# Weight bits put together in a PSUM bank, head pairs 5 to 7 on one bank by groups, and small VectorE work of pairs 4 to 7 on ScalarE

## The chip, the cores and the metric

One NeuronCore of a Trainium2 chip runs the whole kernel. Its engines work side by side, each through its own queue in order: TensorE (PE in the profile; PEld is its weight loads), VectorE (DVE), ScalarE (ACT), GpSimd (POOL) and the load queue of SyncE (SP). The metric is the device time of one execution in microseconds; the median of the runs counts.

## The reference

Three stages follow each other. Causal attention in a window comes first (4 batches, 8 heads, 576 positions, 64 values a head; heads 0 to 3 see 32 positions, heads 4 to 7 every fourth of 128). Its output, 2304 tokens of 512 values, goes through a first layer whose weights are float64, and then through a layer of 8 experts of which each token uses two.

```python
scores = scale * np.matmul(q, k.transpose(0, 1, 3, 2))
scores = np.where(masks[None, :, :, :], scores, -1000000000.0)
...
attn = attn / (np.sum(attn, axis=-1, keepdims=True) + 1e-09)
x = np.matmul(attn, v)        # then as 2304 tokens of 512
...
h = x @ w_in                  # w_in, w_out are float64
g = h * np.cos(h)
x = g @ w_out
...
noisy_logits = logits + noise_scale * noise
top2 = np.argpartition(-noisy_logits, 2, axis=1)[:, :2]
...
        h = np.maximum(x[mask] @ w1[e], 0.0)
        out[mask] += top2_w[mask, k, None] * (h @ w2[e])
```

## The kernel before

**Attention** works on 16 head pairs (`u`), 4 for each batch. A pair's queries lie block-diagonal, so one product serves both heads. `a_scores` writes a pair's masked scores as two groups of 5 and 4 blocks of 96 columns, each in one PSUM bank (`sc`), and takes the row maxima (L442), scaled by -0.125 (L444). `a_exp` makes the nine exponentials on ScalarE (L459) and their sums, `a_norm` divides (L470, L471, GpSimd L473). `a_part` has three parts: two transpose groups of three blocks (`mt`, copied out to `at` by L487), then the first half of the output (`mo`) and the third transpose group, then the second output half. The output halves are copied into `xraw` by L512 (plain pairs) or L521 (dilated pairs, which reorder the columns). Pairs 0 to 3 and the scores of pair 4 are done in an opening stretch; pairs 4 to 7 lie beside the first layer's steps 0 to 15.

**The first layer** takes blocks of 256 tokens and eighths `p` of the hidden width; a step is one such pair. Steps 0 to 15 serve blocks 0 and 1 in turn, so that a new weight tile is needed every second step; from step 16 on the weights stay. A step is 24 products `ph` (`g1`, L561), then `post` on the other engines (ScalarE L569, VectorE L570, ScalarE Sin L572 and Square L573, VectorE L574, ScalarE L577, GpSimd L578), and 12 products `acc` (`g2`, L588) in two halves that use the result of two steps earlier.

**The weights.** The chip has no float64, so the two 32-bit words of each weight are loaded and cut to float32. A weight tile has four quarters of 128x512. For each, `w_bits` makes three VectorE passes over integers: L289 takes exponent and upper bits out of the high word, L290 puts the sign in, L291 puts in the top of the low word. Their result is the SBUF tile `cut`. Then `w_parts` makes the two parts that TensorE multiplies: a rounded copy on ScalarE (L297) and the remainder on GpSimd (L298).

**PSUM** has eight banks: four for `acc`, two for `ph`, and two (`mid`) that the scores of pairs 5 and on, the transposes and the outputs of pairs 4 and on take in turn.

**The order** is written out by hand. `OPENING` lists the opening stretch. `BESIDE` lists for each step what is issued at its positions: -1 behind `g1`, 0 and 1 behind the first half of `g2` with a stage of `post` after each, 2 behind the second half. Every engine's queue follows this order.

## Time and profile before

| | us |
|---|---|
| median of 3 runs | 1040.83 (1040.08 to 1043.03) |
| span of the profiled execution, first to last instruction | 1039.2 |
| TensorE busy in it | 991.0 |
| VectorE busy | 551.7 |
| ScalarE busy | 461.8 |
| GpSimd busy | 369.4 |

The profiled execution's own time is known as its span; the runs of the table were timed apart from it, and their median lies 1.6 us above. Busy time of an engine can overlap that of the others, so the rows don't add up to the span. PE's busy share is an average over the opening stretch, the first layer (to about 550 us) and the experts, which have different limits.

### The profile page before, as it was taken

The page shows a single profiled execution, that of the slowest core. Times are in us where ns is not written, and L with a number is a line of the kernel's source. Part 1 is how long each engine was busy: PE and PEld are TensorE (multiplying, and loading weights), DVE is VectorE, ACT ScalarE, POOL GpSimd, SP SyncE. Part 2 cuts the span into 40 slices and gives each one's busy share as a digit, 9 for nine tenths or more (in the row PEclk, how much of TensorE's full clock was granted, in tenths as well). Part 3 has the DMA queues.
Part 4 walks back from the last instruction along what each step waited for, and adds up shares of the span by engine and source line. Part 5 has one row for each costly group of instructions (what it writes and reads, how often), then busy time and mean ns, then how long its engine had stood idle before and what let it go on. Part 6 is the DMA issues. An engine that isn't in the chain of part 4 may idle for free.

```text
span 1039.2 us, 16801 instructions
## 1 busy us (share of the span) xinstructions
PE 991.0 (95%) x6560; PEld 879.4 (85%) x6560; DVE 551.7 (53%) x1134; ACT 461.8 (44%) x908; POOL 369.4 (36%) x477
## 2 busy tenths in 40 slices
PE   8787889999999899999999899999999999999995
PEld 6676778988889789888887799898998989898984
DVE  7799885367745645354474656353443435353221
ACT  6646665555646655455564334232332314142110
POOL 5555553243353342423425332322313142323211
PEclk9898999999999999999999899999999999999998
DMA  9962212223312120000145154443533342441201
GB/s 208 334 210 86 80 55 43 85 71 113 95 52 57 46 48 1 21 19 4 35 179 179 26 176 136 159 149 135 166 110 138 123 152 79 163 142 59 64 28 41
DMA packets 70842, 105.71 MB, mean 102 GB/s; under 512 B 31364, under 2 KB 44932, under 8 KB 70753
## 3 DMA queue, kind: packets, MB, share of 16 engines
q1 hardware_dynamic: 60400, 76.33, 24.1%
q0 software_dynamic: 10352, 28.20, 8.7%
q8 instruction: 54, 0.88, 0.4%
q14 instruction: 36, 0.29, 0.1%
HBM read 86.40 MB, written 20.11 MB: 102 GB/s over the span
## 4 chain that ended last, share of the span: by engine, by line
PE 75%; DVE 10%; DMA 5%; ACT 5%; issue 2%; SPq 2%; POOL 1%; POOLq 0%; ACTq 0%; DVEq 0%
PE ye L932 21%; PE pe L899 20%; PE ph L561 14%; PE acc L588 13%; DMA raw<-in_wm 3%; DVE cut L290 2%; PE mgx L882 2%; PE sc L429 1%; PE mo L504 1%; DVE r L570 1%; DVE po L653 1%; PE mt L484 1%; DMA ahead<-in_v 1%; ACT s L459 1%; ACT r L573 1%
## 5 line engine op out<-in xcount | busy, mean ns | idle before, releaser
L561 PE MATMUL ph<-xhl,wm 128*128 128x256 f32 x1728 | 229.5, 289 | 11.4 <-ACT wm L297 4.1
L561 PEld LDWEIGHTS ph<-xhl,wm 128*128 128x128 f32 x1728 | 219.0, 195 | 19.8 <-ACT wm L297 4.5
L932 PE MATMUL ye<-we,h 128*128 128x512 f32 x960 | 232.5, 399 | 0.0
L588 PE MATMUL acc<-wm,g 128*128 128x512 f32 x864 | 219.9, 398 | 2.7 <-POOL wm L298 0.9
L932 PEld LDWEIGHTS ye<-we,h 128*128 128x128 f32 x960 | 179.8, 190 | 39.1
L588 PEld LDWEIGHTS acc<-wm,g 128*128 128x128 f32 x864 | 156.5, 190 | 33.4 <-POOL g L578 1.2
L578 POOL TENSOR_TENSOR g<-r,g 128x512 fp32r<-128x512 f32 x72 | 95.8, 1330 | 209.0 <-ACT g L577 208.9
L899 PE MATMUL pe<-xga,we 128*128 128x384 f32 x768 | 135.9, 335 | 0.0
L899 PEld LDWEIGHTS pe<-xga,we 128*128 128x128 f32 x768 | 132.9, 188 | 0.5 <-issue 0.4
L944 POOL DMA_INDIRECT out<-old,tir x35 | 35.9, 1025 | 232.3 <-DVE old L942 227.8
L902 DVE SCALAR_TENSOR_TENSOR h<-pe,h 128x256 fp32r<-128x256 f32 (+1 forms) x128 | 62.8, 491 | 104.3 <-ACT h L901 103.4
L901 ACT ACTIVATE h<-pe 128x256 fp32r<-128x256 f32 (+1 forms) x128 | 56.1, 438 | 128.7 <-PE pe L899 128.7
L942 DVE SCALAR_TENSOR_TENSOR old<-ye,wts,old 128x512 f32<-128x512 f32 x35 | 26.3, 751 | 134.4 <-PE ye L932 134.4
L899 PE MATMUL pe<-xgb,we 128*128 128x256 f32 x768 | 94.3, 283 | 0.1
L899 PEld LDWEIGHTS pe<-xgb,we 128*128 128x128 f32 x768 | 93.3, 191 | 0.4 <-DVE xgb L885 0.4
L574 DVE SCALAR_TENSOR_TENSOR r<-r,ph 128x512 f32<-128x512 f32 x72 | 49.4, 687 | 82.2 <-ACT r L573 82.1
L570 DVE SCALAR_TENSOR_TENSOR r<-r,ph 128x512 f32<-128x512 int32 x72 | 49.2, 683 | 81.7 <-ACT r L569 81.7
L819 DVE TENSOR_TENSOR we<-wraw,we 128x512 fp32r<-128x512 f32 x121 | 84.3, 705 | 3.6 <-ACT we L818 0.9
L818 ACT ACTIVATE we<-wraw 128x512 fp32r<-128x512 f32 x128 | 78.4, 623 | 2.6 <-issue 2.6
L572 ACT ACTIVATE r<-r 128x512 f32<-128x512 f32 x72 | 45.5, 632 | 65.7 <-DVE r L570 65.6
L569 ACT ACTIVATE r<-ph 128x512 int32<-128x512 f32 x72 | 42.6, 592 | 50.6 <-PE ph L561 50.0
L577 ACT ACTIVATE g<-r 128x512 fp32r<-128x512 f32 x72 | 45.5, 632 | 43.8 <-DVE r L574 29.8
(181 smaller groups left out, 1039.1 us busy)
## 6 DMA issues: line engine op xcount, KB each, us to landing
wraw<-in_we SPq DMA_DIRECT2D x64, 512.0 KB, 5.9
raw<-in_wm SPq DMA_DIRECT2D x28, 512.0 KB, 9.3
vts<-in_v SPq DMA_DIRECT2D x13, 384.0 KB, 3.9
x1d<-x SPq DMA_DIRECT2D x9, 512.0 KB, 3.2
out<-zt SPq DMA_DIRECT2D x18, 256.0 KB, 4.0
kts<-in_kT SPq DMA_DIRECT2D x13, 288.0 KB, 3.4
qts<-in_qT SPq DMA_DIRECT2D x26, 144.0 KB, 3.8
piece<-in_wm SPq DMA_DIRECT2D x4, 512.0 KB, 4.8
```

The costliest lines, as they stand in the source:

```text
L561: nc.tensor.matmul(ph[:, j, :], w[:, a, o:o + P], t[:, x, c, :], start=(c == 0 and n == 0 and (j == 0 or len(cs) == 4)), stop=(c == 3 and ...
L570: nc.vector.scalar_tensor_tensor(r, n, -TWO_PI, ph, op0=ALU.mult, op1=ALU.add)
L572: nc.scalar.activation(r, r, AF.Sin, scale=0.5)
L574: nc.vector.scalar_tensor_tensor(r, r, 0.5, ph, op0=ALU.subtract, op1=ALU.mult)
L578: nc.gpsimd.tensor_tensor(g[:, 1, :], r, g[:, 0, :].bitcast(F32), op=ALU.subtract)
L588: nc.tensor.matmul(ACC[blk][t], g[:, a, j * TB + t * P:j * TB + (t + 1) * P], w[:, x, 1024 + j * DM:1024 + (j + 1) * DM], start=(p == 0 an ...
L818: nc.scalar.activation(t[:, 0, fs], raw, AF.Copy)
L819: eng.tensor_tensor(t[:, 1, fs], raw, t[:, 0, fs].bitcast(F32), op=ALU.subtract)
L899: nc.tensor.matmul(ph[:, :n], w[:, a, o:o + P], x[:, b, c, :], start=(c == 0 and i == 0), stop=(c == 3 and i == 2))
L901: nc.scalar.activation(h[:, 0, f, :], ph[:, :n], AF.Relu)
L902: nc.vector.scalar_tensor_tensor(h[:, 1, f, :], ph[:, :n], 0.0, h[:, 0, f, :].bitcast(F32), op0=ALU.max, op1=ALU.subtract)
L932: nc.tensor.matmul(acc, h[:, a, f, o:o + P], w[:, b, (f % 4) * DM:(f % 4 + 1) * DM], start=(f == 0 and i == 0), stop=(f == 7 and i == 2))
```

## The change

In steps 0 to 15, the stretch marked by the list `alone`, one of the two `mid` banks is given to `w_bits`. Its first two passes then write the bits to this bank (`bits`), and the third reads them there and writes `cut` in SBUF. In the opening and from step 16 on, the two banks go in turn to whoever asks (`mid_tile`), as the two buffers did, and the bits of the four quarters made in the opening stay in SBUF. In steps 0 to 15 everything else that used the two banks has one. The scores and exponentials of pairs 5 to 7 are issued by group (`a_s`, `a_e`), so that the second group's products can stand behind the first group's exponentials. For pairs 4 to 7 the scaling of the maxima and both output copies are issued on ScalarE.

```diff
+    turn = [0]
+    alone = []
+    def mid_tile(name):
+        turn[0] += not alone
+        return psum.tile([P, 512], F32, tag="mid" if alone or turn[0] % 2 else "cut", name=name, bufs=1)
...
-        V.tensor_scalar(t, hw, 3, 0x3FFFFFF8, op0=ALU.logical_shift_left, op1=ALU.bitwise_and)
-        V.scalar_tensor_tensor(t, hw, 0xC0000000, t, op0=ALU.bitwise_and, op1=ALU.bitwise_or)
-        V.scalar_tensor_tensor(t, lw, 29, t, op0=ALU.logical_shift_right, op1=ALU.bitwise_or)
+        b = psum.tile([P, 512], F32, tag="cut", name=f"bits{j}_{k}", bufs=1).bitcast(U32) if alone else t
+        V.tensor_scalar(b, hw, 3, 0x3FFFFFF8, op0=ALU.logical_shift_left, op1=ALU.bitwise_and)
+        V.scalar_tensor_tensor(b, hw, 0xC0000000, b, op0=ALU.bitwise_and, op1=ALU.bitwise_or)
+        V.scalar_tensor_tensor(t, lw, 29, b, op0=ALU.logical_shift_right, op1=ALU.bitwise_or)
...
-    def a_scores(u):
+    def a_scores(u, gs=(0, 1)):
...
-            sc = psum.tile([P, 512], F32, tag=tag, name=f"sc{u}_{g}", bufs=bufs)
+            if u > 4:
+                sc = mid_tile(f"sc{u}_{g}")
+            else:
+                tag, bufs = ("ph", 2) if u == 2 else ("acc", 4)
+                sc = psum.tile([P, 512], F32, tag=tag, name=f"sc{u}_{g}", bufs=bufs)
...
-                nc.vector.tensor_scalar(mx[:, i0:i1], mx[:, i0:i1], -0.125, None, op0=ALU.mult)
+                if u < 4:
+                    nc.vector.tensor_scalar(mx[:, i0:i1], mx[:, i0:i1], -0.125, None, op0=ALU.mult)
+                else:
+                    nc.scalar.activation(mx[:, i0:i1], mx[:, i0:i1], AF.Copy, scale=-0.125)
...
-        mid = psum.tile([P, 512], F32, tag="mid", name=f"mt{u}_{c}", bufs=2)
+        mid = mid_tile(f"mt{u}_{c}")
...
-            a_av(u, 0)
+            a_av(u, 0, u < FUSED)
             a_trans(u, 2)
         else:
-            a_av(u, 1)
+            a_av(u, 1, u < FUSED)
...
+        if i == 0:
+            alone.append(True)
+        if i == 16:
+            alone.clear()
...
-8:0 a_loadv(6) w_parts(4,3) w_bits(5,0) a_scores(6)
-8:1 a_loadqk(7) w_bits(5,1) w_parts(5,0) a_exp(6) a_norm(6) w_parts(5,1) w_piece(7,0) w_bits(5,2)
+8:0 a_loadv(6) w_parts(4,3) w_bits(5,0) a_s(6,0) a_e(6,0)
+8:1 a_s(6,1) a_loadqk(7) w_bits(5,1) w_parts(5,0) a_e(6,1) a_norm(6) w_parts(5,1) w_piece(7,0) w_bits(5,2)
```

What this does to the queues is shown at three places. The number at the end of a name counts buffers and differs between the kernels; `[waits ...]` names the engines whose signal an instruction waits for.

TensorE at the scores of pair 6, step 8 (`sc_0` and `sc_1` are the two groups, `acc_1` the second half of `g2`). Before:

```order
L420 MATMUL sc_0_1233<-mask_113,identb 128x480 [waits PE_49]
L429 MATMUL sc_0_1233<-kts,qts 128x96 [waits DMAHW4_49,DMAHW3_49,DMAHW2_49]
L429 MATMUL sc_0_1233<-kts,qts 128x96 x4
L420 LDWEIGHTS identb
L420 MATMUL sc_1_1242<-mask_113,identb 128x384 [waits DVE_49]
L429 MATMUL sc_1_1242<-kts,qts 128x96 x4
L588 MATMUL acc_1_721<-wm_898,g_3_1083 128x512 x6
```

Now:

```order
L438 MATMUL sc_0_1250<-mask_113,identb 128x480 [waits Activation_49]
L447 MATMUL sc_0_1250<-kts,qts 128x96 [waits DMAHW4_49,DMAHW3_49,DMAHW2_49]
L447 MATMUL sc_0_1250<-kts,qts 128x96 x4
L438 LDWEIGHTS identb [waits DVE_49]
L438 MATMUL sc_1_1268<-mask_113,identb 128x384 [waits Activation_49]
L447 MATMUL sc_1_1268<-kts,qts 128x96 x4
L609 MATMUL acc_1_725<-wm_906,g_3_1096 128x512 x6
```

The order of the products is the same for pairs 6 and 7; the second group waits for VectorE's maximum and for ScalarE's exponentials of the first. For pair 5 alone the six `acc` products moved between the groups.

TensorE at the first transposes of pair 6, behind step 9 (`mt_0` and `mt_1` are the transpose groups, `ph_5` the next step's `g1`). Before:

```order
L484 MATMUL mt_0_1345<-ident,s_1231 96x128 [waits Activation_49,Pool_49]
L484 MATMUL mt_0_1345<-ident,s_1231 96x128 x2
L484 MATMUL mt_1_1351<-ident,s_1231 96x128 [waits DVE_49,Activation_49,Pool_49]
L484 MATMUL mt_1_1351<-ident,s_1231 96x128 x2
L561 MATMUL ph_5_1356<-xhl_448,wm_1226 128x256 [waits DVE_49]
```

Now:

```order
L505 MATMUL mt_0_1365<-ident,s_1248 96x128 [waits Activation_49,Pool_49]
L505 MATMUL mt_0_1365<-ident,s_1248 96x128 x2
L505 MATMUL mt_1_1371<-ident,s_1248 96x128 [waits Activation_49,Pool_49]
L505 MATMUL mt_1_1371<-ident,s_1248 96x128 x2
L582 MATMUL ph_5_1376<-xhl_448,wm_1242 128x256 x8
```

Nothing moved here; the ScalarE signal that `mt_1` waits for was that of the second score group's exponentials, and is now the copy of `mt_0`, the last user of the bank.

ScalarE from the exponentials of pair 6 (`s` from `sc`) on, step 8. Before:

```order
L459 ACT_TABLE_LOAD
L459 ACTIVATE s_1231,sm_1262<-sc_0_1233,mx_1232 128x96 x5
L459 ACTIVATE s_1231,sm_1262<-sc_1_1242,mx_1232 128x96 x4
L297 ACTIVATE wm_1226<-cut_1_1256 128x512
L577 ACTIVATE g_4_1285<-r_4_1213 128x512
L569 ACTIVATE r_4_1319<-ph_4_1294 128x512
L572 ACT_TABLE_LOAD
```

Now:

```order
L465 ACTIVATE mx_1249<-mx_1249 128x5
L481 ACT_TABLE_LOAD
L481 ACTIVATE s_1248,sm_1259<-sc_0_1250,mx_1249 128x96 x5
L593 ACT_TABLE_LOAD
L593 ACTIVATE r_4_1229<-r_4_1229 128x512
L594 ACTIVATE r_4_1229<-r_4_1229 128x512
L465 ACTIVATE mx_1249<-mx_1249 128x4
L307 ACTIVATE wm_1242<-cut_0_1243 128x512
L481 ACT_TABLE_LOAD
L481 ACTIVATE s_1248,sm_1259<-sc_1_1268,mx_1249 128x96 x4
L307 ACTIVATE wm_1242<-cut_1_1279 128x512
L598 ACTIVATE g_4_1304<-r_4_1229 128x512
```

Sin and Square of step 8 (now L593, L594), which stood ahead of all nine exponentials, stand between the two groups; the table load ahead of the next step's Sin follows in both kernels, so pairs 6 and 7 have four loads each in place of two.

## Rows read from the trace of the kernel before

**Rows 1.** The page's first line, and TensorE's part of its first section.

```profile
span 1039.2 us, 16801 instructions
...
PE 991.0 (95%) x6560; PEld 879.4 (85%) x6560; DVE 551.7 (53%) x1134; ACT 461.8 (44%) x908; POOL 369.4 (36%) x477
```

**Rows 2.** Table of stretches: from:to and length, busy us by engine, granted clock, DMA.

```profile
43.00:69.00 26.00, 21.83 (x149) 18.32 (x150) 24.66 (x31) 11.64 (x21) 16.09 (x12) 0.86 0.73 222
69.00:105.00 36.00, 30.24 (x195) 26.50 (x195) 32.42 (x39) 21.93 (x49) 19.03 (x15) 0.91 0.39 129
105.00:125.00 20.00, 16.66 (x124) 14.19 (x123) 17.48 (x28) 13.77 (x36) 10.98 (x10) 1.00 0.36 103
125.00:138.00 13.00, 11.81 (x107) 10.14 (x107) 11.43 (x16) 5.78 (x11) 8.19 (x6) 1.00 0.00 1
138.00:168.00 30.00, 27.61 (x199) 23.51 (x198) 23.39 (x37) 20.91 (x48) 16.19 (x14) 1.00 0.35 84
```

**Rows 3.** List by line, ScalarE, 43 to 168: busy us, mean ns, idle before.

```profile
L297 ACT ACTIVATE wm<-cut 128x512 fp32r<-128x512 f32 x28 | 17.8, 636 | 36.0 <-DVE cut L291 36.0
```

**Rows 4.** Two lines' durations (ns, min/median/max), and the timeline at 94 us.

```profile
L289 DVE TENSOR_SCALAR cut<-raw x28: 366/420/1527, 22.3 to 142.0; 128x512 uint32<-128x512 uint32 x28
L290 DVE SCALAR_TENSOR_TENSOR cut<-raw,cut x28: 691/1368/1690, 22.7 to 142.5; 128x512 uint32<-128x512 uint32 x28
...
94.27 1.34 POOL L298 TENSOR_TENSOR wm<-cut,wm 128x512 fp32r<-128x512 f32 x1 [2.02 <-ACT wm L297]
94.49 1.67 DVE L290 SCALAR_TENSOR_TENSOR cut<-raw,cut 128x512 uint32<-128x512 uint32 x1
```

**Rows 5.** List by line, VectorE, 43 to 168: the three passes of the bits.

```profile
L290 DVE SCALAR_TENSOR_TENSOR cut<-raw,cut 128x512 uint32<-128x512 uint32 x24 | 31.2, 1301 | 0.8
L291 DVE SCALAR_TENSOR_TENSOR cut<-raw,cut 128x512 uint32<-128x512 uint32 x24 | 24.4, 1016 | 0.8
L289 DVE TENSOR_SCALAR cut<-raw 128x512 uint32<-128x512 uint32 x23 | 14.7, 639 | 0.0
```

**Rows 6.** Durations of line 574, which reads one operand from PSUM.

```profile
L574 DVE SCALAR_TENSOR_TENSOR r<-r,ph x72: 675/688/692, 44.0 to 549.0; 128x512 f32<-128x512 f32 x72
```

**Rows 7.** ScalarE by line, 43 to 168, and the durations of its line 521.

```profile
L487 ACT ACTIVATE at<-mt 96x384 f32<-96x384 f32 x12 | 5.3, 477 | 2.0 <-PE mt L484 2.0
L459 ACT ACT_TABLE_LOAD x3 | 3.8, 1283 | 0.4 <-DVE mx L444 0.4
...
L521 ACT COPY xraw<-mo x4: 666/696/766, 26.7 to 37.6; 128x288 f32<-128x288 f32 x4
```

**Rows 8.** Timelines of TensorE, VectorE and ScalarE at pair 6: start, us, instruction.

```profile
108.52 1.25 PE L429 MATMUL sc<-kts,qts 128*128 128x96 f32 x10
...
110.67 1.63 PE L588 MATMUL acc<-wm,g 128*128 128x512 f32 x6
112.13 3.04 PE L561 MATMUL ph<-xhl,wm 128*128 128x256 f32 x24
115.01 2.91 PE L588 MATMUL acc<-wm,g 128*128 128x512 f32 x12
119.53 0.53 PE L484 MATMUL mt<-ident,s 128*96 128x128 f32 x3 [1.61 <-POOL s L473]
...
112.96 0.65 DVE L442 TENSOR_REDUCE mx<-sc 128x5 f32<-128x480 f32 x1
...
115.19 0.34 ACT L459 ACTIVATE s<-sc,mx 128x96 f32<-128x96 f32 x1
116.69 0.22 ACT L459 ACTIVATION_READ_ACCUMULATOR s<-sc,mx 128x1 f32 x1
```

**Rows 9.** TensorE's wait at 84 us, and two stretches at the lower clock.

```profile
84.11 0.63 PE L561 MATMUL ph<-xhl,wm 128*128 128x256 f32 x2 [3.30 <-ACT wm L297]
...
63.84:67.25 3.41, 3.30 (x13) 2.71 (x11) 3.34 (x4) 0.63 (x1) 1.91 (x2) 0.50 0.80 180
84.32:91.14 6.82, 6.09 (x23) 5.35 (x23) 5.41 (x5) 4.40 (x7) 5.45 (x6) 0.50 0.04 13
```

## What I predict, and from what

> **What bounds the kernel now.** I read the page first: TensorE (PE) is busy for 95% of the 1039.2 us span [rows 1], so a microsecond saved on another engine counts only where PE waits for that engine. The table of stretches then shows where PE waits. From 43 to 168 us, which is the first layer's steps 2 to 15 with head pairs 4 to 7 beside them, PE is idle for 4.17 + 5.76 + 3.34 + 1.19 + 2.39 = 16.85 us [rows 2]. The reader should see VectorE (DVE) in the same rows: 24.66 + 32.42 + 17.48 + 11.43 + 23.39 = 109.4 us busy out of 125. The list by line names the chain. ScalarE (ACT) sat idle for 36.0 us ahead of its L297 copies, waiting for VectorE's L291 [rows 3]. GpSimd's L298 follows L297, and the first product of the next weights follows that. So in this stretch VectorE's weight bits set the pace, and PE feels them two engines later. Nothing of the change lies behind step 16.
>
> **The weight bits.** Each quarter of a weight tile takes three VectorE passes over 128x512. L290 takes 691 ns at best and 1690 at worst [rows 4]. The two rows of one moment show why: a GpSimd subtraction (L298) ran from 94.27, and L290, begun at 94.49, took 1.67 us [rows 4]. The means in the stretch are 639 (L289), 1301 (L290) and 1016 ns (L291) [rows 5], 2.96 us for the three. After the change each of them reads at most one SBUF tile. No row shows a VectorE pass that writes PSUM. The nearest is L574, which reads one operand from PSUM and one from SBUF: 72 of them between 675 and 692 ns, also beside GpSimd [rows 6]. I price all three at 0.69: 2.07 us. L289 could stay at its present median of 0.42 (lower bound), and all three could be as dear as today (upper bound, a rival below). For the 28 quarters that is 28 x (2.96 - 2.07) = 24.9 us less VectorE work. The scalings (L444) of pairs 4 to 7 and the copies of their outputs leave VectorE too, so it falls from 109 to under 85 us of 125 and stops being the bound.
> The first pass is where I weighed a rule. L289 reads and writes SBUF alone and takes 366 to 420 ns when undisturbed, where L290 needs 691 [rows 4]. The Trainium skill, VectorE: DVE Perf Modes, section Why PSUM operands drop a tier, says that a float32-sized pass with an operand in PSUM runs at one element a cycle only. By the rule L289 rises to L574's 0.69; by the row alone it stays at 0.42, and two of the pauses below are each 0.27 us shorter.
>
> **What ScalarE gets.** Eight scalings, the copies of both halves of four pairs, and four more loads of its function table: for pairs 6 and 7 the exponentials now come in two groups with Sin and Square between them. A table load is 1.283 us [rows 7], so 5.1 us. The copies are bounded by the one ScalarE copy of such an output, 0.696 for a dilated half [rows 7]; cut in two pieces I take 0.95 for pairs 6 and 7, and 0.4 to 0.6 for pairs 4 and 5: 5.8 us. With 0.2 for a scaling (estimate, from the 0.22 us of the accumulator's read at 116.69 [rows 8]) ScalarE has 12.5 us more than its 74 us of 125 [rows 2]. It isn't full, but its queue is in order, and that decides the next part.
>
> **The one bank.** This is the term that decides. In steps 0 to 15 every transpose group, output and score group of pairs 4 to 7 takes the same bank, so PE may not begin the next before the last has been read out, and whatever PE has queued behind waits too: the next g1 block and with it the whole step. Three kinds of pause come of it.
> First, the second score group waits for the five exponentials of the first. Before, PE wrote both groups in one go: from 108.52, with the next block's products at 110.67 already [rows 8]. For pair 6 the chain from ScalarE's first pass of step 8 is 0.6 + L570 0.69 + bits 2.07 + maximum 0.65 (112.96 [rows 8]) + scaling 0.2 + table 1.28 + five exponentials 1.72 (115.19 to 116.91 [rows 8]) = 7.2 us. PE has 2.1 us of work beside it (the rest of six products and the first group), so the pause is 5.1. For pair 7 no bits stand ahead of the maximum: 0.65 + 0.2 + 1.28 + 1.72 and 0.1 of latency, 4.0. For pair 5 the six products moved between the groups (1.46 us, 110.67 to 112.13 [rows 8]) come off, but 1.6 us of bits and L574 stand ahead: 4.2.
> Second, the transposes of blocks 3 to 5 wait for the copy of blocks 0 to 2, which stands on ScalarE behind the step's post work. For pair 6, counted from the end of the five exponentials: table 1.28, Sin and Square 1.27, L574 0.69, maximum 0.6, scaling 0.2, L297 0.64 [rows 3], table 1.28, four exponentials 1.38, L297 0.64, L577 0.64, L569 0.6, table 1.28, Sin and Square 1.27, L574 0.69, L577 0.64, the copy 0.48 (L487 [rows 7]): 13.6 us. PE has the second group 1.0, six products 1.46, a g1 block 2.88, twelve products 2.9 and a transpose group 0.3 beside it, 8.5 (the steps between the PE rows of [rows 8]): a pause of 5.0. In the same way I get 3.3 for pair 4, 0.8 for pair 5 and 1.5 for pair 7.
> Third, the last transposes wait for the copy of the first output half: 2.7, 2.4, 2.5 and 1.9 for pairs 4 to 7, since that copy stands behind Sin, Square and (pairs 4 and 5) L577 of the step.
> Together 13.3 + 10.6 + 9.5 = 33.4 us in 11 pauses. The least that the waits can be, with ScalarE free and VectorE at hand, is 2.4 + 3.9 + 3.9 for the scores, four times 0.75 for the transposes and four times 0.9 for the outputs: 16.8 us.
>
> **The rest.** Pairs 5 to 7's scores by group add no matmul. From step 16 on the two banks serve by turns, as the two buffers did before. The orders of GpSimd and of the load queue (SP) stay. On SP the loads of a pair's values and keys wait for PE's products as before and move with PE; the pieces of the last weights wait for VectorE, which is earlier.
>
> **The sum.** The 33.4 us are counted from issue to issue; the trace counts idle time only after the last product's end, which for a transpose group is 0.53 us after its start [rows 8] against a step of 0.29. So 33.4 - 11 x 0.25 = 30.6 us of idle time. Off it come the 16.85 us of idle time of before (all, since the weights are then ready: an assumption that favours the change) and the clock that was lost. A wait of 3.30 us, until 84.11, was followed by 6.82 us in which the granted clock was 0.50, the lower of its two levels (1.2 GHz) [rows 9]; one more such stretch of 3.41 us lies at 63.84. At half rate they cost (6.83 + 3.41) / 2 = 5.1 us. So 30.6 - 16.85 - 5.1 = +8.7. Five of the new pauses are as long as that one or longer. After three of them (pair 5's and 7's scores, pair 6's transposes) PE's own work sets the pace; elsewhere ScalarE's chain hides a slow PE. Each may cost 0 to 3.4 us, 0 to 10.2 together; I take one, 3.4. That is +12.1 us: a span of 1051.3. The median of the runs (1040.83) stands 1.6 above the profiled span, which I leave as it is: 1053 us.
>
> **The rivals.** (a) Faster: ScalarE, no longer waiting 36 us for L291 [rows 3], has its copies done as soon as PE writes, and the pauses are at their least. Then 16.8 - 2.7 - 16.85 - 5.1 = -7.9: 1033. It decides once the pauses sum to less than about 22 us. For it speaks that ScalarE's idle time ahead of L297 is the largest wait here; against it that the copies stand behind a chain which starts only when PE's own g1 block ends, whatever VectorE does.
> (b) No change: the pauses come to some 25 us and no slow clock follows them: 22.2 - 16.85 - 5.1 = +0.3, 1041. For it: after 115.01 PE waited for the pair's transposes anyway until 119.53 [rows 8], so some pauses fall into time that was lost before.
> (c) The change doesn't do what it says: passes that write PSUM are as dear as today's 2.96 us. Then the pauses stay and half of the old waits do too: 30.6 - 8.4 - 5.1 + 5 = +22, 1063. Against it stand L574's 72 even times [rows 6]. The Trainium skill, SBUF — State Buffer, section Who interferes with whom, says that a VectorE pass with at most one SBUF input, outside its two-port modes, doesn't contend with GpSimd; by that rule (c) is out, and L574's rows agree with it, but none of them writes PSUM.
>
> **How the numbers follow.** Forecast (slower, around 1053) 0.64; (a) 0.22; (b) 0.10; (c) 0.04. The range takes in (a)'s floor and the three slow stretches at full price (+18.9, 1060) with some of (c): 1033 to 1062. Over 0.3% (3.1 us, about what a measurement of this kernel can tell from no change) slower: 0.64 + 0.04 = 0.68; same 0.10; faster 0.22.
>
> **What would show it.** The three passes at 0.6 to 0.7 us each with a narrow spread, and VectorE at 75 to 85 us in the stretch, show the first step. PE waits of 4 to 5 us between the score groups of pairs 6 and 7 and of about 5 ahead of pair 6's second transposes, each ended by ScalarE, show the second; four more table loads show the ScalarE term; lengthened stretches at 0.50 behind these pauses show the clock term. The prediction is wrong if PE's idle time in steps 2 to 15 is below 22 us: then ScalarE was free when the bank's readers were due.

## The result, and the profile of the changed kernel

The changed kernel takes 1052.68 us (median of 4 runs, 1052.25 to 1053.04), beside 1041.93 (1040.08 to 1043.19) for the kernel before in runs of the same set: 1.0109 times as long, with a 95% interval of 1.0093 to 1.0126. The forecast was 1053.0, slower. In a later set the ratio was 1.0122 (1.0096 to 1.0149).

The first rows are those of the page of after, which answer to [rows 1].

```profile
span 1050.5 us, 16827 instructions
...
PE 992.8 (95%) x6560; PEld 884.8 (84%) x6560; DVE 523.2 (50%) x1112; ACT 472.4 (45%) x934; POOL 362.0 (34%) x477
```

The span is 11.3 us longer than before. The table of stretches of after answers to [rows 2]: from:to and length, then busy us of PE, PEld, DVE, ACT and POOL, the granted clock, the DMA share and GB/s.

```profile
43.00:69.00 26.00, 22.16 (x156) 18.89 (x154) 20.40 (x33) 15.43 (x29) 15.89 (x14) 0.87 0.73 224
69.00:105.00 36.00, 29.60 (x215) 26.24 (x214) 22.60 (x37) 22.40 (x53) 17.22 (x15) 0.95 0.36 124
105.00:125.00 20.00, 11.64 (x67) 10.34 (x67) 10.81 (x19) 14.32 (x35) 7.34 (x8) 0.91 0.34 100
125.00:138.00 13.00, 11.21 (x84) 10.30 (x85) 6.47 (x11) 5.86 (x12) 4.97 (x5) 0.87 0.01 2
138.00:168.00 30.00, 25.31 (x164) 22.48 (x162) 13.44 (x23) 20.44 (x46) 13.00 (x12) 0.89 0.32 70
```

Fixed times are a poor ruler here, because the two kernels aren't at the same place at 168 us. A better one runs from the first products of step 2 (those that wait for GpSimd's `xhl`, at 42.89 us before and 42.70 after) to pair 7's last output (161.59 and 172.44). Both stretches hold the same work: 710 and 711 recorded matmuls. I call this **the common stretch**. The table of stretches gives one row of before for it:

```profile
42.89:161.59 118.70, 101.85 (x710) 86.89 (x710) 103.18 (x140) 70.69 (x156) 66.25 (x52) 0.94 0.42 124
```

and one of after:

```profile
42.70:172.44 129.74, 103.39 (x711) 90.73 (x711) 77.04 (x123) 81.04 (x178) 58.42 (x52) 0.91 0.37 112
```

It is 11.04 us longer, so nearly all of the 11.3 lies in it. PE is busy 1.54 us more and idle 129.74 - 103.39 = 26.35 us instead of 118.70 - 101.85 = 16.85, that is 9.50 more. VectorE has 26.1 us less to do, ScalarE 10.4 more.

**The bits got cheap.** The durations (min/median/max in ns) of the three passes in after, against [rows 4] and [rows 5]:

```profile
L299 DVE TENSOR_SCALAR bits<-raw x24: 676/686/695, 41.6 to 142.8; 128x512 uint32<-128x512 uint32 x24
...
L300 DVE SCALAR_TENSOR_TENSOR bits<-raw,bits x24: 695/696/697, 42.3 to 143.5; 128x512 uint32<-128x512 uint32 x24
...
L301 DVE SCALAR_TENSOR_TENSOR cut<-raw,bits x24: 686/687/689, 43.1 to 144.3; 128x512 uint32<-128x512 uint32 x24
```

Together they take 2.07 us, and they are even. ScalarE's list by line shows that the old chain is gone: its `wm` copies, which stood idle for 36.0 us behind VectorE [rows 3], now wait 5.6.

```profile
L307 ACT ACTIVATE wm<-cut 128x512 fp32r<-128x512 f32 x26 | 16.3, 626 | 5.8 <-DVE cut L301 5.6
```

**The bank got dear.** The list of PE's waits in after, 43 to 180 us (line waited for: us in total, times, longest):

```profile
PE sc L438 <- ACT s L481: 8.8, 2, 4.8
PE mt L505 <- ACT at L508: 7.9, 4, 3.6
PE sc L443 <- ACT s L481: 3.9, 1, 3.9
PE mt L505 <- ACT xraw L542: 3.1, 2, 1.8
PE mt L505 <- ACT xraw L533: 2.6, 2, 1.8
```

Every one is a wait for ScalarE to read the one bank out. They are 11 pauses and sum to 26.3 us, the whole idle time of the common stretch. (The list has one line more, the wait for `xhl`, which had ended at 42.70, where the stretch begins.) The timeline of PE in after has the second score groups of pairs 5, 6 and 7 and pair 6's second transposes, with the pause in brackets:

```profile
75.84 0.32 PE L443 MATMUL sc<-mask,identb 128*128 128x384 bf16 x1 [3.92 <-ACT s L481]
76.00 1.02 PE L447 MATMUL sc<-kts,qts 128*128 128x96 f32 x8
...
111.27 0.48 PE L438 MATMUL sc<-mask,identb 128*128 128x384 bf16 x1 [4.79 <-ACT s L481]
111.54 1.86 PE L447 MATMUL sc<-kts,qts 128*128 128x96 f32 x8
...
120.92 0.49 PE L505 MATMUL mt<-ident,s 128*96 128x128 f32 x3
124.98 0.85 PE L505 MATMUL mt<-ident,s 128*96 128x128 f32 x3 [3.57 <-ACT at L508]
125.48 4.38 PE L582 MATMUL ph<-xhl,wm 128*128 128x256 f32 x24
...
135.48 3.03 PE L582 MATMUL ph<-xhl,wm 128*128 128x256 f32 x24
...
146.17 0.48 PE L438 MATMUL sc<-mask,identb 128*128 128x384 bf16 x1 [4.03 <-ACT s L481]
```

The same eight score products take 1.02 us at 76 us and 1.86 at 111.54, and the same 24 projections 4.38 and 3.03. The rows of stretches of after tell why: around and behind the longer pauses the granted clock was 0.50, the lower of the two levels (1.2 GHz).

```profile
111.30:114.70 3.40, 3.40 (x13) 3.11 (x13) 0.85 (x2) 2.47 (x3) 0.00 (x0) 0.50 0.11 10
124.90:128.30 3.40, 3.32 (x16) 3.33 (x17) 0.86 (x2) 0.49 (x1) 0.98 (x1) 0.50 0.01 2
145.40:152.20 6.80, 6.03 (x22) 5.45 (x22) 3.14 (x5) 5.49 (x15) 0.00 (x0) 0.50 0.00 1
```

With two more stretches of 3.4 us, from 53.2 and from 77.1 (0.51), that makes 20.4 us at half rate at the five pauses of 3.01 to 4.79 us. The length of a pause doesn't decide it alone: in e10, the same kernel again, 3.4 us at 0.50 from 103.2 on followed a pause of 1.81 us, and behind the same pause in after the clock stayed at 1.00. Before, [rows 9] had 10.2 us inside the stretch, and 3.8 more stood at its start (3.4 after).

### The profile page after: what moved, and what is told of

Same layout as the page of the kernel before. It is cut to its first block, busy times and chain, and to the rows that moved or that the text cites. A ratio compares the mean times of both kernels' runs of the same rounds, so it can differ in the third digit from the quotient of the medians.

```text
span 1050.5 us, 16827 instructions
## 1 busy us (share of the span) xinstructions
PE 992.8 (95%) x6560; PEld 884.8 (84%) x6560; DVE 523.2 (50%) x1112; ACT 472.4 (45%) x934; POOL 362.0 (34%) x477
## 4 chain that ended last, share of the span: by engine, by line
PE 78%; DVE 8%; ACT 6%; DMA 2%; issue 2%; SPq 2%; POOL 1%; ACTq 0%; DVEq 0%; POOLq 0%
PE pe L929 21%; PE ye L962 20%; PE ph L582 17%; PE acc L609 14%; PE sc L447 2%; PE mgx L912 2%; PE mo L525 1%; PE mt L505 1%; DVE po L674 1%; ACT r L594 1%; ACT r L593 1%; DMA ahead<-in_v 1%; PE mx L633 1%; DVE r L591 1%; DVE r L595 1%
## 5 line engine op out<-in xcount | busy, mean ns | idle before, releaser
L599 POOL TENSOR_TENSOR g<-r,g 128x512 fp32r<-128x512 f32 x72 | 92.8, 1289 | 220.7 <-ACT g L598 217.5
L595 DVE SCALAR_TENSOR_TENSOR r<-r,ph 128x512 f32<-128x512 f32 x72 | 49.4, 686 | 98.0 <-ACT r L594 97.9
L591 DVE SCALAR_TENSOR_TENSOR r<-r,ph 128x512 f32<-128x512 int32 x72 | 49.2, 683 | 95.7 <-ACT r L590 95.7
L972 DVE SCALAR_TENSOR_TENSOR old<-ye,wts,old 128x512 f32<-128x512 f32 x35 | 26.3, 751 | 134.4 <-PE ye L962 134.4
L593 ACT ACTIVATE r<-r 128x512 f32<-128x512 f32 x72 | 45.4, 630 | 59.8 <-DVE r L591 59.6
```

The costliest lines, as they stand in the source:

```text
L591: nc.vector.scalar_tensor_tensor(r, n, -TWO_PI, ph, op0=ALU.mult, op1=ALU.add)
L593: nc.scalar.activation(r, r, AF.Sin, scale=0.5)
L595: nc.vector.scalar_tensor_tensor(r, r, 0.5, ph, op0=ALU.subtract, op1=ALU.mult)
L599: nc.gpsimd.tensor_tensor(g[:, 1, :], r, g[:, 0, :].bitcast(F32), op=ALU.subtract)
```

## The experiments

**How they are compared.** The opening, of which the edits touch little (the scaling of pair 4's maxima), turned out to differ from execution to execution (last section), so beside the medians I give each kernel's common stretch, read from its own table of stretches. How far this ruler can be trusted is seen where one kernel was traced twice: after and e10 have 129.74 and 129.94 us, but e3 and e11 135.64 and 133.82. A difference of some 2 us on it, taken from one trace each, therefore shows little. Each ratio is to the runs of before in the kernel's own set, whose medians lay between 1041.01 and 1042.74.

| kernel | median us | ratio to before, 95% interval | common stretch | PE idle | VectorE busy |
|---|---|---|---|---|---|
| before | 1041.93 | | 118.70 | 16.85 | 103.18 |
| after | 1052.68 | 1.0109 (1.0093 to 1.0126) | 129.74 | 26.35 | 77.04 |
| e1 one bank, bits in SBUF | 1069.17 | 1.0246 (1.0224 to 1.0269) | 145.49 | 35.46 | 98.86 |
| e2 small work on VectorE | 1061.47 | 1.0186 (1.0169 to 1.0204) | 138.62 | 32.59 | 84.64 |
| e3 exponentials together | 1058.35 | 1.0149 (1.0130 to 1.0168) | 135.64 | 29.03 | 77.04 |
| e4 two banks, 19 quarters in PSUM | 1037.26 | 0.9953 (0.9936 to 0.9970) | 114.57 | 14.75 | 85.05 |
| e5 small work alone | 1044.85 | 1.0027 (1.0015 to 1.0038) | 119.94 | 17.79 | 99.26 |
| e6 two banks, 14 quarters | 1030.54 | 0.9877 (0.9860 to 0.9893) | 109.71 | 10.67 | 90.15 |
| e7 second scores later | 1057.35 | 1.0133 (1.0110 to 1.0157) | 133.60 | 30.12 | 77.17 |
| e8 two banks, 12 quarters | 1032.76 | 0.9924 (0.9907 to 0.9942) | 111.71 | 14.79 | 92.56 |
| e9 e7, transposes later | 1057.88 | 1.0151 (1.0117 to 1.0184) | 135.21 | 30.70 | 77.03 |
| e10 after, again | 1055.27 | 1.0122 (1.0096 to 1.0149) | 129.94 | 25.71 | 77.03 |
| e11 e3, again | 1056.32 | 1.0140 (1.0118 to 1.0163) | 133.82 | 28.25 | 77.05 |

### The parts one by one: e1 and e5

e1 is the changed kernel with the bits in SBUF:

```diff
-        b = psum.tile([P, 512], F32, tag="cut", name=f"bits{j}_{k}", bufs=1).bitcast(U32) if alone else t
+        b = psum.tile([P, 512], F32, tag="cut", name=f"bits{j}_{k}", bufs=1).bitcast(U32) if False else t
```

> The changed kernel, but the bits of the weights stay in SBUF in all steps; the one bank for scores, transposes and outputs, and the small work on ScalarE, are kept. Theory (the one bank makes TensorE wait for ScalarE's readers, and the bits in PSUM soften that): VectorE is again near 100 us busy in steps 2 to 15, the maxima come later, the pauses grow, 1060 to 1072 us. Rival (writing bits to PSUM is itself what costs): the time comes back to 1040 to 1046 us.

e5 is the kernel before with nothing but the small work moved:

```diff
-                nc.vector.tensor_scalar(mx[:, i0:i1], mx[:, i0:i1], -0.125, None, op0=ALU.mult)
+                if u < 4:
+                    nc.vector.tensor_scalar(mx[:, i0:i1], mx[:, i0:i1], -0.125, None, op0=ALU.mult)
+                else:
+                    nc.scalar.activation(mx[:, i0:i1], mx[:, i0:i1], AF.Copy, scale=-0.125)
...
-            a_av(u, 0)
+            a_av(u, 0, u < FUSED)
...
-            a_av(u, 1)
+            a_av(u, 1, u < FUSED)
```

> The kernel before with only one part of the change: the scaling of the maxima and the copies of the output for pairs 4 to 7 go to ScalarE; two banks and the bits in SBUF stay. Theory (the single bank makes the loss, ScalarE has room): this costs little, 1039 to 1046 us, and TensorE's waits stay those of before, under 6 us in sum. Rival (ScalarE's added work makes the loss): 1047 to 1053 us, with waits for ScalarE's activations and copies over 12 us in sum between 43 and 168 us.

Both times fell where the theory put them. (The waits of e5 were put wrongly, at under 6 us: before has 16.85 us of idle time already, and e5 has 17.79.) On the common stretch the change then comes apart in three steps, each put on top of the last: small work +1.24 (before to e5, within what two traces of one kernel can differ), the single bank and its order by groups +25.55 (e5 to e1), the bits in PSUM -15.75 (e1 to after), in sum +11.04. In e1's list by line VectorE's second pass is again about as dear as before the change, 1221 ns where after has 696:

```profile
L300 DVE SCALAR_TENSOR_TENSOR cut<-raw,cut 128x512 uint32<-128x512 uint32 x24 | 29.3, 1221 | 0.8
```

and in its list of PE's waits the same readers of the bank are waited for, for longer, and next to nothing else is. For pair 5 the timeline of VectorE in e1 has longer bits ahead of the maximum: from 78.69 on L591, then three passes of 0.42, 1.66 and 0.69 us, L595 and the maximum at 82.64.

```profile
PE sc L438 <- ACT s L481: 10.1, 2, 5.5
...
PE sc L443 <- ACT s L481: 5.9, 1, 5.9
...
PE acc L609 <- POOL wm L308: 0.5, 1, 0.5
```

Only 0.5 us of e1's 35.46 us of idle time is a wait for a weight, though its bits are as heavy as before: with one bank PE comes late enough that the weights are ready anyway. So what the lighter bits bring here is a shorter way round the bank, 9.11 us of idle time and 6.64 us of PE's busy time. And the bank costs more than they bring.

### Is it ScalarE's load? e2, e3 and e11

e2 puts the scalings and the output copies back on VectorE, everything else as in after:

```diff
-                if u < 4:
+                if u < FUSED:
...
-            a_av(u, 0, u < FUSED)
+            a_av(u, 0)
...
-            a_av(u, 1, u < FUSED)
+            a_av(u, 1)
```

> The changed kernel with the scaled maxima and the output copies of pairs 4 to 7 back on VectorE; one bank and bits in PSUM are kept. Theory: the pauses at the scores and at the second transposes stay, those ahead of the third transposes (0.83 + 1.81 + 1.79 + 1.27 us, which wait for the output copies on ScalarE) shrink to under 1 us each: 1047 to 1052 us. Rival (ScalarE's added work, not the bank, is what costs): 1040 to 1045 us.

Both expected ranges were missed: it is 8.9 us slower than after on the common stretch. The timeline of PE in e2 shows pair 4's third transposes:

```profile
60.77 0.85 PE L505 MATMUL mt<-ident,s 128*96 128x128 f32 x3 [6.13 <-DVE xraw L533]
```

and the timeline of VectorE in e2 what stood ahead of the copy that frees the bank:

```profile
58.70 0.69 DVE L300 SCALAR_TENSOR_TENSOR bits<-raw,bits 128x512 uint32<-128x512 uint32 x1
59.50 0.69 DVE L301 SCALAR_TENSOR_TENSOR cut<-raw,bits 128x512 uint32<-128x512 uint32 x1
60.11 0.52 DVE L533 COPY xraw<-mo 128x192 f32<-128x192 f32 x2
```

VectorE has no gap of more than 0.1 us there. From 54.64, when PE began to wait, six passes of bits and L595 stand ahead of the copy, and the bank is held all that time. So the move of the small work to ScalarE, which gains nothing alone (+1.24 us), is worth 8.9 us once there is only one bank.

e3 issues both score groups' exponentials of pairs 6 and 7 ahead of the step's Sin, so that four table loads go:

```diff
-8:0 a_loadv(6) w_parts(4,3) w_bits(5,0) a_s(6,0) a_e(6,0)
-8:1 a_s(6,1) a_loadqk(7) w_bits(5,1) w_parts(5,0) a_e(6,1) a_norm(6) w_parts(5,1) w_piece(7,0) w_bits(5,2)
+8:0 a_loadv(6) w_parts(4,3) w_bits(5,0) a_s(6,0) a_e(6,0) a_s(6,1) w_parts(5,0) a_e(6,1)
+8:1 a_loadqk(7) w_bits(5,1) a_norm(6) w_parts(5,1) w_piece(7,0) w_bits(5,2)
...
-11:0 w_parts(6,2) a_s(7,0) w_bits(6,3) a_e(7,0)
-11:1 a_s(7,1) a_e(7,1) w_bits(7,0) w_parts(6,3)
+11:0 w_parts(6,2) a_s(7,0) w_bits(6,3) a_e(7,0) a_s(7,1) a_e(7,1)
+11:1 w_bits(7,0) w_parts(6,3)
```

> The changed kernel with both exponential groups of pairs 6 and 7 ahead of Sin and Square of the step, so that ScalarE loads its table four times less (5.1 us); one bank kept. Theory: the pauses at the second score groups (4.8 and 4.0 us) stay as they are, that ahead of pair 6's second transposes (3.57 us) loses some 2.6: 1048 to 1052 us. Rival (the table loads on ScalarE are what costs): 1040 to 1046 us.

Missed again: 1058.35. Part of that was in front of the edit, since e3's step 2 began at 45.29 instead of 42.70. So the changed kernel and e3 ran once more side by side.

> The changed kernel itself once more, beside e11 on one chip, to separate the opening from the change's own stretch. Theory (whether the products of the opening, up to 43 us, fall into the granted clock of 0.50 varies from execution to execution or from chip to chip, by 2 to 6 us, whatever the edit): 1050 to 1060 us, with first products of step 2 between 42.5 and 45.5 us; from there to pair 7's last output 129.7 us, as in the first profile. Rival (the opening belongs to the kernel): 1052 to 1053 us again and the same opening.

> e3_exps_together once more on the same chip. Theory (its loss lay in front of the edit): it ends within 3 us of e10, if both have the same opening, and the table loads saved give nothing. Rival (the edit itself costs): 5 to 7 us above e10 again, with the second transposes of pair 6 waiting over 4.4 us.

e10 came out as its theory had it. This time the openings were the other way round: step 2 began at 45.43 us in e10 and at 41.07 in e11. The medians lie 1 us apart, which agrees with the theory's 3 us, but the openings weren't the same, as it had asked for, so the totals prove nothing. On the common stretch e11 is 3.9 us above e10 and e3 5.9 above after. That is less than the rival's 5 to 7 us for the first of the two, but the edit itself costs, as the rival had it, and the pause that it named grew. ScalarE is busy 5 us less in both (75.94 against 80.84 and 81.04), and the time still goes up. The timeline of ScalarE in e3 shows where:

```profile
119.93 0.21 ACT L465 ACTIVATE mx<-mx 128x4 f32<-128x4 f32 x1 [2.81 <-DVE mx L460]
...
122.01 1.28 ACT L593 ACT_TABLE_LOAD   x1
```

ScalarE's queue stands for 2.81 us in front of the second maximum, which itself waits for PE's second score group. Behind it stand Sin, Square and the copy that releases the next transposes. Here is that copy's waiter in the timeline of PE in e11:

```profile
127.66 0.85 PE L505 MATMUL mt<-ident,s 128*96 128x128 f32 x3 [4.67 <-ACT at L508]
```

In after it waited 3.57 us, in e10 2.92. Of the 3.9 us between e10 and e11 this pause makes 1.75, a new wait of pair 6's first transposes for GpSimd 0.79, and PE's busy time the rest. The saved table loads buy nothing: ScalarE is not full, and what PE waits for stands behind a wait in ScalarE's queue.

### Is it PE's order? e7 and e9

e7 lets PE do other products during the way round: the second score groups of pairs 5, 6 and 7 come one or two positions later.

```diff
-4:2 w_bits(3,1) a_s(5,1)
-5:-1 a_e(5,1) w_parts(3,1) w_load(5,0) a_norm(5) w_load(5,1) w_bits(3,2)
-5:0 w_load(5,2)
-5:1 w_load(5,3) w_parts(3,2) w_load(6,0)
+4:2 w_bits(3,1)
+5:-1 w_parts(3,1) w_load(5,0) w_load(5,1) w_bits(3,2)
+5:0 a_s(5,1) w_load(5,2)
+5:1 a_e(5,1) a_norm(5) w_load(5,3) w_parts(3,2) w_load(6,0)
...
-8:1 a_s(6,1) a_loadqk(7) w_bits(5,1) w_parts(5,0) a_e(6,1) a_norm(6) w_parts(5,1) w_piece(7,0) w_bits(5,2)
+8:1 w_bits(5,1) w_parts(5,0) w_parts(5,1) w_piece(7,0) w_bits(5,2)
+9:-1 a_s(6,1) a_loadqk(7)
+9:0 a_e(6,1) a_norm(6)
...
-11:1 a_s(7,1) a_e(7,1) w_bits(7,0) w_parts(6,3)
-12:-1 a_norm(7)
-12:0 w_bits(7,1) w_parts(7,0) w_piece(7,2)
+11:1 w_bits(7,0) w_parts(6,3)
+12:-1 a_s(7,1)
+12:0 a_e(7,1) a_norm(7) w_bits(7,1) w_parts(7,0) w_piece(7,2)
```

> The changed kernel with the second group of scores of pairs 5, 6 and 7 issued one or two positions later on TensorE (and its exponentials and normalisation after it). Theory (the three pauses of 3.92, 4.79 and 4.03 us are the way from scores over maxima, scaling and five exponentials back to the one bank, and TensorE stands behind a waiting instruction although other products are ready): they fall below 1.5 us each, less of the span has the granted clock of 0.50, 1036 to 1046 us. Rival (the lost time is ScalarE's work, or it moves to the transposes, which come right behind a later normalisation): 1049 to 1056 us.

The three pauses did go, all but 0.5 us. The list of PE's waits of e7 shows what came in their place:

```profile
PE mt L507 <- POOL s L496: 14.2, 4, 8.9
...
PE sc L440 <- ACT s L483: 0.5, 1, 0.5
```

The transposes now come right behind the later normalisation on GpSimd, as the rival said; the time, 1057.35, lies 1.35 us above even the rival's range. e9 therefore moves the first transposes one position later as well:

```diff
-6:0 a_part(5,0) w_bits(4,0) w_parts(3,3)
-6:1 w_parts(4,0)
+6:0 w_bits(4,0) w_parts(3,3)
+6:1 a_part(5,0) w_parts(4,0)
...
-9:2 a_part(6,0)
-10:0 w_parts(5,2)
+10:0 a_part(6,0) w_parts(5,2)
...
-13:0 a_loadqk(8) a_part(7,0)
+13:0 a_loadqk(8)
+13:1 a_part(7,0)
```

> As e7_later_scores, with the first transposes of pairs 5, 6 and 7 one position later too, so that the normalisation on GpSimd has time to end. Theory (with one bank the lost time is the way there and back, wherever TensorE comes upon it too early): the 13.5 us of waits of the transposes for the normalised scores fall below 5, 1040 to 1050 us. Rival (the pair's work is too long for the time between its scores and its use, so that the wait only moves on to the projections): 1052 to 1060 us.

The wait for GpSimd fell from 14.2 to 5.1 us, and the time stayed, 1057.88, in the rival's range. The list of PE's waits of e9:

```profile
PE mt L507 <- ACT at L510: 16.7, 4, 5.8
PE mt L507 <- POOL s L496: 5.1, 3, 2.4
```

So the wait moved on, though not to the projections, as the rival had it: it went to the second transposes. For pair 7, whose wait is the longest, the timeline of ScalarE in e9 has the table load, Sin and Square of two steps ahead of the copy. Two orders were tried, and PE's idle time was 30.1 and 30.7 us instead of 26.35. Whether some other order lets one bank break even stays open.

### Is it the bank? e4, e6 and e8

These keep the order of before, its small work on VectorE, and both banks for the pairs, one by role: the second score group and the later transposes (`sc1`, `mt1`, `mt2`) in one bank, the rest in the other. The bits share the first of these banks, except for quarters whose turn there would collide; those are made in SBUF as before. e4 is this, with 9 quarters in SBUF:

```diff
+    INSBUF = {(2, 2), (3, 0), (3, 1), (4, 3), (5, 0), (5, 1), (6, 2), (6, 3), (7, 0)}
+
+    def mid_tile(name, second=False):
+        turn[0] += not alone
+        return psum.tile([P, 512], F32, tag="cut" if (second if alone else turn[0] % 2) else "mid", name=name, bufs=1)
...
+        b = psum.tile([P, 512], F32, tag="cut", name=f"bits{j}_{k}", bufs=1).bitcast(U32) if alone and (j, k) not in INSBUF else t
+        V.tensor_scalar(b, hw, 3, 0x3FFFFFF8, op0=ALU.logical_shift_left, op1=ALU.bitwise_and)
+        V.scalar_tensor_tensor(b, hw, 0xC0000000, b, op0=ALU.bitwise_and, op1=ALU.bitwise_or)
+        V.scalar_tensor_tensor(t, lw, 29, b, op0=ALU.logical_shift_right, op1=ALU.bitwise_or)
```

> The kernel of before with its order and its small work on VectorE; both banks serve pairs 4 to 7 (the first score group, the first transposes and the outputs in one, the rest in the other), and 19 of the 28 quarters' bits use the second bank where no pair holds it; the other nine stay in SBUF. Theory: no pause for a lone bank, and some 17 us less on VectorE take away part of the 16.85 us of waits and of the slow clock: 1030 to 1038 us. Rival (bits in PSUM gain nothing, the waits of before had another cause): 1040 to 1044 us. If the bits and the pairs get in each other's way in the shared bank: over 1044 us.

1037.26 us, faster than both kernels, as the theory had it. (The banks by role and the bits in one of them came together; the roles alone, with all bits in SBUF, weren't run, so how the gain divides between the two isn't shown.) One line is left in its list of PE's waits that matters:

```profile
PE mt L495 <- DVE cut L299: 14.2, 5, 5.6
```

The transposes wait for the third pass of bits in the shared bank. e6 takes the five quarters ahead of those transposes out of the bank:

```diff
-    INSBUF = {(2, 2), (3, 0), (3, 1), (4, 3), (5, 0), (5, 1), (6, 2), (6, 3), (7, 0)}
+    INSBUF = {(1, 3), (2, 1), (2, 2), (3, 0), (3, 1), (3, 3), (4, 3), (5, 0), (5, 1), (5, 2), (5, 3), (6, 2), (6, 3), (7, 0)}
```

> As e4_both_banks, but five more quarters (those whose bits stood in the shared bank just ahead of the transposes that waited 14.2 us for them) are put together in SBUF; 14 of 28 quarters stay in PSUM. Theory (the bank shared in time is what costs, and only where a holder is followed by a waiter): most of the 14.2 us of waits goes, VectorE has some 4 us more work, 1028 to 1035 us. Rival (VectorE needs all of the lighter passes): the weights come later and TensorE waits for the copies wm instead, 1037 to 1043 us.

1030.54 us: inside the theory's range, 1.2% faster than before. The wait for the bits fell from 14.2 to 7.7, though VectorE has 5.1 us more to do. e6's list of PE's waits:

```profile
PE mt L495 <- DVE cut L299: 7.7, 2, 4.2
```

The durations of the second pass in e6 show both places of the bits in one execution:

```profile
L298 DVE SCALAR_TENSOR_TENSOR cut<-raw,cut x17: 691/693/1687, 23.3 to 135.6; 128x512 uint32<-128x512 uint32 x17
L298 DVE SCALAR_TENSOR_TENSOR bits<-raw,bits x11: 695/695/697, 42.9 to 127.8; 128x512 uint32<-128x512 uint32 x11
```

e8 adds the two quarters that the remaining 7.7 us wait for:

```diff
-    INSBUF = {(1, 3), (2, 1), (2, 2), (3, 0), (3, 1), (3, 3), (4, 3), (5, 0), (5, 1), (5, 2), (5, 3), (6, 2), (6, 3), (7, 0)}
+    INSBUF = {(1, 3), (2, 0), (4, 2), (2, 1), (2, 2), (3, 0), (3, 1), (3, 3), (4, 3), (5, 0), (5, 1), (5, 2), (5, 3), (6, 2), (6, 3), (7, 0)}
```

> As e6_both_banks_14, and the two quarters for whose bits the third transposes of pairs 4 and 5 still waited 4.20 and 3.54 us are put together in SBUF too; 12 of 28 quarters stay in PSUM. Theory (the wait is for the holder ahead in the shared bank): these 7.7 us go, and part of the granted clock of 0.50 behind them, for 0.6 us more work on VectorE, 1022 to 1028 us. Rival (VectorE is behind at both places, and the transposes would have waited for their own copies anyway): 1029 to 1034 us.

The time is the rival's, 1032.76, and no better than e6's: the ratios to before are 0.9924 and 0.9877, and the common stretch is 2.0 us longer, no more than two traces of one kernel can differ. The wait for the bits fell to 1.7 us, but in the timeline of PE in e8 pair 4's last outputs wait instead:

```profile
64.93 1.33 PE L515 MATMUL mo<-at,vts 96*64 96x32 f32 x20 [7.57 <-DVE xraw L523]
```

and the timeline of VectorE in e8 shows passes in SBUF ahead of the copy that they wait for, four of them at 1.63 us or more between 54 and 64:

```profile
58.32 1.63 DVE L298 SCALAR_TENSOR_TENSOR cut<-raw,cut 128x512 uint32<-128x512 uint32 x1
...
62.72 1.64 DVE L299 SCALAR_TENSOR_TENSOR cut<-raw,cut 128x512 uint32<-128x512 uint32 x1
64.28 0.51 DVE L523 COPY xraw<-mo 128x192 f32<-128x192 f32 x2
```

So each of the two costs was seen once: with 19 quarters in the bank PE waits for the holder, with 12 VectorE is late. Which quarters are taken out matters as well as how many, and only three choices were run. e6 is the best of them and of all kernels here.

## Why the prediction came true, step by step

**The bits: right.** 0.69 us for each pass, and the rows read 686, 696 and 687 ns. The lower bound, L289 at its present 0.42, is out. The Trainium skill, VectorE: DVE Perf Modes, section Why PSUM operands drop a tier, says that a float32-sized pass with a PSUM operand runs at one element a cycle. The trace agrees for a pass that only writes PSUM: 412 ns (median of the four in the opening, SBUF to SBUF) became 686.

**Rival (c), passes as dear as today: out.** The 24 second passes lie between 695 and 697 ns, while e1's second passes, in SBUF, average 1221. The Trainium skill, SBUF — State Buffer, section Who interferes with whom, has contention between VectorE and GpSimd over the shared ports only; e6's two rows agree, 695 to 697 ns with the bits in PSUM and 691 to 1687 with them in SBUF.

**VectorE: right in size, the saving on the bits put a little high.** 26.1 us less on the common stretch: 3.9 by the small work (before to e5), 21.8 by the bits (e1 to after), where the prediction had 24.9 for the bits and left the small work without a number. From 43 to 168 us it reads 73.7 where 75 to 85 was forecast, as these fixed times hold less of the work now.

**ScalarE: a little less.** 10.4 us more instead of 12.5. The four table loads came (5 and 5 in the stretch where 3 and 3 were) and the scalings take 208 ns. The copies were priced from the 696 ns of a dilated half; e5's list by line has 1.7 + 2.6 us for 14 pieces, where 5.8 us had been put for all.

**The eleven pauses: right in kind and place, too long in sum.** Idle time, forecast (issue to issue less 0.25) against the trace of after:

| | pair 4 | pair 5 | pair 6 | pair 7 |
|---|---|---|---|---|
| second scores | none | 3.95 / 3.92 | 4.85 / 4.79 | 3.75 / 4.03 |
| second transposes | 3.05 / 3.01 | 0.55 / 0.67 | 4.75 / 3.57 | 1.25 / 0.67 |
| third transposes | 2.45 / 0.83 | 2.15 / 1.81 | 2.25 / 1.79 | 1.65 / 1.27 |

Eight of eleven are within 0.5 us. Forecast 30.6, measured 26.4. Pair 6's second transposes show how the miss came about. The chain on ScalarE was put at 13.6 us from the end of the exponentials, 111.23; the timeline of ScalarE in after has the copy at its end:

```profile
124.37 0.47 ACT L508 ACTIVATE at<-mt 96x384 f32<-96x384 f32 x1
```

It ends at 124.84, 13.6 us later, to the tenth. What was wrong is the work beside it: 8.5 us was put, and it lasted from 111.27 until 121.21 (the last transposes' start at 120.92 and their step of 0.29), 9.9 us, because PE had the lower clock from 111.3 to 114.7. A slow PE fills its own pause. The same holds for the largest miss, pair 4's third transposes. The timeline of PE in after has these products ahead of them, at the lower clock:

```profile
53.04 2.73 PE L609 MATMUL acc<-wm,g 128*128 128x512 f32 x6
```

The output half that follows took 1.19 us. At full clock such products take 1.63 and 0.77 (at 89.68 and 96.87), 1.5 us less in all, and the miss is 1.62.

**The clock: too small.** The step put 5.1 us of old loss off and took one new stretch of 3.4 us out of bounds of 0 to 10.2, net -1.7. The rows at 0.50 came to 20.4 us where 10.2 stood. By the prediction's own rule, half of such a stretch is lost, that is 10.2 in place of 5.1: the upper bound, net +5.1. To choose 3.4 out of the bounds had no row behind it.

PE's busy time rose by only 1.54 us, so without the clock it would have fallen by some 3.5. In part this is because before broke blocks of products up: in its timeline 24 projections, begun at 100.13 at full clock, came in three pieces of 0.96, 0.50 and 2.17 us, 3.63 together, where 24 in one go take 3.03. The rest is open.

**The sum: near, and in part by luck.** Pauses 13.75 forecast against 9.50, the clock term -1.7 against the +1.54 of PE's busy time, sum 12.1 against 11.0. The two mis-sized terms belong together, as the slow clock lengthens PE's work and shortens the pauses that this work covers; they largely cancelled. The last step to 1053.0 was luck too: the forecast stands on 1040.83 for before, and the set of the result had 1041.93, so that the difference of the medians is 10.75 us where 12.1 was forecast, and the two times still agree to 0.3. Kind, place and direction were understood; the agreement to a third of a microsecond was not earned.

**The old waits: gone, but not by the bits alone.** The prediction took all 16.85 us of old idle time off, since lighter bits would have the weights ready. None of it is left in after. But e1 has heavy bits and only 0.5 us of waits for weights: a PE that is late itself is enough.

**Rival (a), ScalarE free in time: out,** on its own point of decision: 26.35 us of idle time, not under 22. Half of what spoke for it came true (ScalarE's wait for the bits fell from 36.0 to 5.6 us) and what spoke against it decided. e5 shows that the load alone is nearly free, e3 and e11 that less load doesn't help.

**Rival (b), no change: out.** Its 25 us are counted from issue to issue, 22.2 of idle time. The pauses came to 26.4, about halfway between that and the forecast's 30.6, and slow stretches did follow them, which it had excluded.

**What the prediction didn't price** is how much the lighter bits are worth under one bank: 15.75 us from e1 to after. Its sum needed no such number, as it priced the end state directly.

## What to carry to other kernels

A buffer that frees another engine's time is paid for by whoever used it as the second of two: follow the way from its write to its release through every queue in between, and compare that with the work that the writer has meanwhile. Where the release stood in an in-order queue behind an instruction that waits, making that engine lighter gained nothing (e3, e11). Put only those turns into the shared buffer that no one waits behind: e6, with 14 of 28 quarters and both banks still serving the pairs, gave -1.2%, where a bank given away for all 28 gave +1.1%. Price pauses and the clock that follows them as one term, compare variants over a stretch of equal work, not by totals or by fixed times, and trace one kernel twice to learn what that ruler can tell.

## What the runs showed of the hardware beyond that

**The opening differs between executions of one kernel.** The first products of step 2 began at 42.70 us in the first trace of the changed kernel and at 45.43 in e10, the same kernel; in e3 at 45.29 and in e11, its copy, at 41.07. The rows of the table of stretches for 28 to 32 us, first of e10:

```profile
28.00:32.00 4.00, 4.00 (x39) 3.37 (x38) 1.18 (x3) 3.67 (x10) 2.94 (x4) 0.50 0.98 354
```

and of e11:

```profile
28.00:32.00 4.00, 4.00 (x43) 3.87 (x43) 3.93 (x7) 0.48 (x3) 1.05 (x2) 1.00 1.01 379
```

In the openings that were late (e1, e3, e7, e9, e10, step 2 at 44.24 us or later) the granted clock was 0.50 there (0.58 in e9), and PE had waited 1.25 to 1.98 us for a load of values (`ahead<-in_v`) just before. In the first trace of after it had waited 1.65 and the clock stayed at 1.00, so the wait alone doesn't tell. What sets it is open. The 4.2 us between e3 and e11, one kernel, are as much as several of the effects measured here.

**A change of the function table costs what its row says.** In the timeline of ScalarE in after the load at 111.23 is followed by the next activation at 112.53, 1.30 us later:

```profile
110.99 0.22 ACT L481 ACTIVATION_READ_ACCUMULATOR s<-sc,mx 128x1 f32 x1
111.23 1.28 ACT L593 ACT_TABLE_LOAD   x1
112.53 0.63 ACT L593 ACTIVATE r<-r 128x512 f32<-128x512 f32 x1
```

The Trainium skill, ScalarE: Activation LUTs, section What ACT_TABLE_LOAD costs, adds a drain of some 1.38 us to each switch, 2.66 in all. The trace doesn't show that here: the accumulator's read ahead of the load had ended at 111.21.
